# A three-stage kernel whose first feed-forward trades 16 plain chunk products for sets of seven half-size products

## Chip, cores and metric

The kernel runs on one core of one Trainium2 chip. The metric is the device time of one execution in microseconds (us); lower is better.

## What is computed

```
attn = causal attention of q, k, v (4 x 8 heads, 576 tokens, head size 64) with a
       per-position bias min(0, cum[j] - cum[i]), cum the running sum of max(s, 0)
x = attn as 2304 tokens x 512
h = x @ w_in                          # 512 x 2048
x = (h * cos(h)) @ w_out              # 2048 x 512        first feed-forward
xn = x / rms(x) * rms_g
g = xn @ w_gate; v = xn @ w_val       # 512 x 1536 each   second feed-forward
out = (silu(g) * v) @ w_out2          # 1536 x 512
```

Weights of the feed-forwards arrive as 64-bit numbers; the kernel makes 32-bit ones of them (`value`). A feed-forward operand is held as two parts, a rounded one and the rest (`split`: a copy and a subtraction), and each product is three matmuls: high by high, high by low, low by high.

## The kernel before

**Stages.** Attention runs over 16 pairs of heads. The first feed-forward follows, then the second one's gate and value products, then its output product. `T_FF1`, `T_FF2` and `T_OUT` are the times at which the planner sets them.

**Order.** Every instruction is a `plan.op` with an engine (or a choice of two), a cost and a due time. `Plan.order` walks through them once on the host and writes one fixed order for each engine; on the chip each engine follows its own list and waits on semaphores. All DMAs are issued from SyncE (SP). A buffer is reused in the order in which the code asks for it, so the order of uses of a PSUM bank is fixed too.

**First feed-forward.** Tokens go in blocks of 512 (the last of 256). For each block and each of 16 chunks of 128 hidden columns, a tick: `gemm1` (12 matmuls, L737) writes one bank; ScalarE and VectorE make h * cos(h) of it (`Identity` L855, a subtraction L350, `Sin` L857, a multiplication, then a split); `gemm2` (12 matmuls, L743) adds to four accumulator banks and is due 1.6 ticks after its `gemm1`. All 16 + 16 weight chunks lie split in SBUF: those of `w_in` are made during attention, those of `w_out` at the stage's start. When a block is done, `rms_norm` and `rms_store` normalise it (squares L799, a ones-matmul L815, some tiny VectorE steps, the scaling L834) and store it to DRAM.

**Second feed-forward.** Gate and value products are made with seven half-size products for eight: weight pairs `p` and `p + 6` and two halves of 384 tokens form a 2 x 2 block product. `pair_weights` makes the combinations of weights during the first feed-forward, splits them, and stores both parts to DRAM; `load_w` brings them back. `load_x2` combines and splits the activations. One set is seven products (`product`, L985: 6 matmuls of 384 columns each) into four banks, two groups of four banks taking turns:

```
mm(b1, "11", "11", True, 0)
...
mm(b2, "S2", "T2", True, 1)
...
mm(b4, "S3", "T3", True, 2)
...
mm(b3, "S1", "T1", True, 3)
...
last_product = mm(b1, "12", "21", False, 4)
mm(b4, "22", "T4", False, 5)
mm(b3, "S4", "22", False, 6)
```

ScalarE copies b1 out, and VectorE adds the partial sums of the other banks in SBUF tiles `t1`, `t2`, `t3`. The product that writes b4 a second time has two products between itself and the first writing, and so has that of b3. There are 36 sets. The output product (L1126) is of the same seven-product form, with 256 columns a matmul.

## Time and profile before

| | |
|---|---|
| median of 3 runs | 980.69 us (979.43 to 982.83) |
| profiled execution, its own time | 982.97 us |
| profiled execution, span of instructions | 981.2 us |
| TensorE busy | 975.1 us, 99% |
| VectorE, ScalarE, GpSimd busy | 75%, 54%, 12% |
| DMA | 197.49 MB, 201 GB/s over the span |

The span runs from the first to the last instruction of the profiled execution; its own time is 1.8 us longer. Durations below come from that one execution. A line number is that of `kernel.py`; a helper such as `two` (L350) or `copy` (L339, L342) has one line for all its uses.

### The profile page before, as it was taken

Reading aid. Unit: us, or ns where it says so; the run is one execution under the profiler, and the core shown is the slowest. Engines: PE = TensorE matmul, PEld = TensorE weight load, DVE = VectorE, ACT = ScalarE, POOL = GpSimd, SP = SyncE. Lnnn points to the kernel's source line nnn. Section 1 sums busy time; section 2 is a strip of 40 time slices with the busy share of each in tenths; the row PEclk is TensorE's granted clock in tenths of the full one; section 3 lists DMA queues with packets and bytes.
Section 4 is the critical chain, followed back from the end, with each engine's and each line's share of the span. In section 5 each row is a group of like instructions: output and inputs, shape, how many; then the busy total and the mean of one; then the engine's idle time right before and its main releaser. Section 6 shows DMA issues by size and latency. Waiting matters only on the chain.

```text
span 981.2 us, 17344 instructions
## 1 busy us (share of the span) xinstructions
PE 975.1 (99%) x5792; PEld 844.9 (86%) x5792; DVE 735.3 (75%) x1641; ACT 534.7 (54%) x1200; POOL 116.3 (12%) x244
## 2 busy tenths in 40 slices
PE   9999999999999999999999999999999999999998
PEld 5666666788888888888888999999999999999998
DVE  4778777888798889868756988766566579987651
ACT  4999999765566575555544662321221225665540
POOL 2445443021101110101100000000000000000000
PEclk9999999999999999999999999999999999999999
DMA  7799997344355556565442444746556378998761
GB/s 237 249 294 307 316 309 227 125 150 130 123 219 216 189 198 236 195 217 209 173 155 87 131 177 138 242 137 210 174 168 220 108 216 270 286 322 244 214 189 44
DMA packets 131834, 197.49 MB, mean 201 GB/s; under 512 B 13104, under 2 KB 93888, under 8 KB 131744
## 3 DMA queue, kind: packets, MB, share of 16 engines
q1 hardware_dynamic: 131744, 196.38, 61.8%
q8 instruction: 45, 0.74, 0.3%
q14 instruction: 45, 0.37, 0.1%
HBM read 129.67 MB, written 66.67 MB: 200 GB/s over the span
## 4 chain that ended last, share of the span: by engine, by line
PE 98%; ACT 1%; DVE 0%; issue 0%; POOL 0%; ACTq 0%; DVEq 0%; POOLq 0%
PE bank L985 27%; PE bank L737 21%; PE bank L743 20%; PE bank L1126 14%; PE bank L638 5%; PE bank L604 4%; PE bank L554 4%; PE bank L578 2%; ACT Pb L339 1%; PE bank L724 0%; PE bank L706 0%; PE bank L519 0%; PE bank L714 0%; PE bank L815 0%; DVE e L561 0%
## 5 line engine op out<-in xcount | busy, mean ns | idle before, releaser
L350 DVE TENSOR_TENSOR wk<-wk,bank 128x384 f32<-128x384 f32 (+2 forms) x237 | 130.8, 558 | 114.0 <-PE bank L985 40.6
L737 PE MATMUL bank<-xa,wi 128*128 128x512 f32 (+1 forms) x960 | 213.5, 374 | 0.0
L743 PE MATMUL bank<-wg,wr 128*128 128x512 f32 (+1 forms) x960 | 210.7, 371 | 0.0
L737 PEld LDWEIGHTS bank<-xa,wi 128*128 128x128 f32 x960 | 167.9, 188 | 35.4 <-issue 0.3
L743 PEld LDWEIGHTS bank<-wg,wr 128*128 128x128 f32 x960 | 167.7, 188 | 33.6
L985 PE MATMUL bank<-wr,wg 128*128 128x384 f32 x504 | 116.4, 338 | 0.0
L985 PE MATMUL bank<-wi,wg 128*128 128x384 f32 x504 | 115.0, 336 | 0.0
L350 DVE TENSOR_TENSOR wg<-wk,wg 128x512 fp32r<-128x512 f32 (+1 forms) x137 | 82.6, 624 | 13.0 <-ACT wg L339 10.7
L439 POOL TENSOR_SCALAR wk<-wk 128x512 f32<-128x512 f32 x68 | 53.4, 787 | 327.1 <-ACT wk L436 312.4
L855 ACT ACTIVATE wk<-bank,quarter 128x512 int32<-128x512 f32 x72 | 49.3, 685 | 78.5 <-PE bank L737 68.2
L339 ACT ACTIVATE wg<-wk 128x512 fp32r<-128x512 f32 (+1 forms) x123 | 68.0, 571 | 43.2 <-DVE wk L350 30.5
L985 PEld LDWEIGHTS bank<-wr,wg 128*128 128x128 f32 x504 | 91.3, 188 | 0.0
L985 PEld LDWEIGHTS bank<-wi,wg 128*128 128x128 f32 x504 | 89.5, 188 | 0.4
L1126 PE MATMUL bank<-wi,wr 128*128 128x256 f32 x585 | 73.6, 281 | 0.0
L561 DVE CUSTOM_DVE_ANT_0 e<-bank,ce 128x512 f32<-128x512 f32 (+2 forms) x96 | 49.7, 553 | 30.0 <-PE bank L554 18.8
L589 ACT ACTIVATE e<-e,mn 128x512 f32<-128x512 f32 (+3 forms) x128 | 70.4, 558 | 2.7 <-DVE mn L561 2.7
L339 ACT ACTIVATE wk<-bank 128x384 f32<-128x384 f32 (+2 forms) x48 | 23.0, 509 | 89.3 <-PE bank L985 51.1
L1126 PEld LDWEIGHTS bank<-wi,wr 128*128 128x128 f32 x585 | 71.2, 188 | 0.0
L350 DVE TENSOR_TENSOR wk<-wk 128x256 f32<-128x256 f32 (+2 forms) x143 | 66.7, 498 | 3.5 <-ACT wk L799 3.1
L857 ACT ACTIVATE wk<-wk,half_pi 128x512 f32<-128x512 f32 x72 | 51.9, 723 | 30.9 <-DVE wk L350 30.7
L339 ACT ACTIVATE wr<-wr 128x384 fp32r<-128x384 f32 x108 | 54.3, 522 | 23.4 <-DMA wr<-g 11.0
L350 DVE TENSOR_TENSOR wk<-bank,wk 128x512 f32<-128x512 f32 (+1 forms) x82 | 55.1, 673 | 13.1 <-ACT wk L857 12.9
(123 smaller groups left out, 1440.1 us busy)
## 6 DMA issues: line engine op xcount, KB each, us to landing
wk<-in_w_out_dram SPq DMA_DIRECT2D x28, 512.0 KB, 5.0
wr<-g_S SPq DMA_DIRECT2D x54, 192.0 KB, 3.1
qk<-in_qk_dram SPq DMA_DIRECT2D x16, 608.0 KB, 4.6
w_g<-wg SPq DMA_DIRECT2D x18, 512.0 KB, 3.4
w_v<-wg SPq DMA_DIRECT2D x18, 512.0 KB, 5.2
wr<-g SPq DMA_DIRECT2D x48, 192.0 KB, 4.1
g_S<-wk SPq DMA_DIRECT2D x45, 192.0 KB, 2.4
wk<-in_w_in_dram SPq DMA_DIRECT2D x16, 512.0 KB, 5.9
```

The source lines that it names most:

```text
L339: alts.append(("ACT", (act_p if psum else act_s)(n), lambda: act.activation(o(), i(), AF.Copy, scale=scale)))
L350: return plan.op(on("DVE", dve1(n), lambda: dve.tensor_tensor(out=o(), in0=a(), in1=b(), op=op)), r, w, **kw)
L439: plan.op(on("POOL", 660, lambda: pool.tensor_scalar(out=top().bitcast(F32), in0=top().bitcast(F32), scalar1=0.0, scalar2=1.0, op0=ALU.mul ...
L561: plan.op(on("DVE", dve1(w) + 17, lambda t=t, o=o, w=w, i=i, e=e: dve.tensor_tensor_reduce(out=Es[e]()[:, o:o + w], in0=Sp[e]()[:, o:o + w ...
L589: plan.op(on("ACT", act_s(w) + 187, lambda E=E, o=o, w=w, i=i, c=c: act.activation(E()[:, o:o + w], E()[:, o:o + w], AF.Exp, scale=-1.0, b ...
L638: pe.matmul(X()[64 * e:64 * e + 64, lo:hi], vr()[:kk, e, c, :], p[e], start=(c == 0), stop=(c == jobs[-1][0]))
L737: pe.matmul(h, w[:, a, 128 * k:128 * k + 128], x[k // 2][:, k % 2, c, :blk], start=(n == 0), stop=(n == 11))
L743: pe.matmul(acc[t], w[:, c, 128 * t:128 * t + 128], g[a], start=(first and (a, c) == (0, 0) and t % per == 0), stop=(last and (a, c) == (1 ...
L855: plan.op(on("ACT", act_p(512) + 93, lambda u=u, h=h: act.activation(u().bitcast(I32), h(), AF.Identity, bias=quarter)), [h], [u])
L857: plan.op(on("ACT", 628, lambda u=u: act.activation(u(), u(), AF.Sin, scale=-TWO_PI, bias=half_pi)), [], [u], table="sin", prio=O_SIN)
L985: pe.matmul(bank_()[:, :HALF2], G[i]()[:, u, o + 128 * k:o + 128 * k + 128], xs[k]()[:, c, :], start=(first and n == 0), stop=(n == 5), sk ...
L1126: pe.matmul(bk_()[:, col:col + 256], gs[p // 3]()[:, u, 128 * (p % 3):128 * (p % 3) + 128], w3[p][i]()[:, c, o:o + 256], start=(n == 0), s ...
```

## The change

The first layer of the first feed-forward now takes the seven-product form: chunk pairs `p` and `p + 8` and tokens in 3 blocks of two halves of 384 make 24 sets, in an order that takes the first three pairs through all blocks first. The result, h * cos(h), goes to DRAM unsplit (`g1_d`). The second layer then runs as a stage of its own, plain, in 6 units of 384 tokens: per unit 16 steps of 12 matmuls into four banks, each step's operand loaded from `g1_d` and split just before.

A new `winograd` function, used by both feed-forwards, sums partial products in PSUM: ScalarE copies a bank into another bank (`move`) or VectorE adds into one, and the next product accumulates on top. The SBUF tiles for the partial sums go. Cosine, silu and the gate multiplication run on two neighbouring banks with one instruction of 768 elements.

`w_in` pairs 0 to 2 are combined and split during attention (`pair_in`); pairs 3 to 7 are combined, stored unsplit (`pair_store`) and loaded and split later (`pair_load`). `w_out` is converted and stored during the first layer and split in the second layer's first unit. The weights of the second feed-forward are no longer made during the first one and kept in DRAM: each pair is converted, combined and split when its set comes near (`ff2_weights`), and the output weights between sets (`pair_out`). `load_x` makes the activation combinations, from the attention's result for the first feed-forward and from the normalised one for the second. `rms` follows each unit of the second layer and reads three of its banks until its last step. Planner constants and buffer places change along with it.

```
-    def gemm1(h, w, x, blk):
-        n = 0
-        for k in range(4):
-            for a, c in ((0, 0), (0, 1), (1, 0)):
-                pe.matmul(h, w[:, a, 128 * k:128 * k + 128], x[k // 2][:, k % 2, c, :blk], start=(n == 0), stop=(n == 11))
-                n += 1
-
-    def gemm2(acc, g, w, first, last, per):
-        for a, c in ((0, 0), (0, 1), (1, 0)):
-            for t in range(4):
-                pe.matmul(acc[t], w[:, c, 128 * t:128 * t + 128], g[a], start=(first and (a, c) == (0, 0) and t % per == 0),
-                          stop=(last and (a, c) == (1, 0)), skip_group_check=True)
-
...
-            h, u, g = h_bank(j), u_r.new(), g_r.new()
-            for i, f in enumerate(fs):
-                plan.now = tick_at(k)
-                ticks[k] = plan.op(on("PE", 1450 if n0 == 256 else 2815, lambda i=i, w=w1[f], h=h, x=xs[j], n0=n0: gemm1(
...
-            plan.now = tick_at(k) - LEAD_E
-            plan.op(on("ACT", act_p(512) + 93, lambda u=u, h=h: act.activation(u().bitcast(I32), h(), AF.Identity, bias=quarter)), [h], [u])
-            two(u, lambda u=u: u().bitcast(I32), h, 512, [h], [u], psum=True)
-            plan.op(on("ACT", 628, lambda u=u: act.activation(u(), u(), AF.Sin, scale=-TWO_PI, bias=half_pi)), [], [u], table="sin", prio=O_SIN)
-            two(u, h, u, 512, [h], [u], op=ALU.mult, psum=True)
-            copy(lambda g=g: g()[:, 0, :], u, 512, [u], [(g, 0)])
-            two(lambda g=g: g()[:, 1, :], u, lambda g=g: g()[:, 0, :].bitcast(F32), 512, [u, (g, 0)], [(g, 1)])
...
+    def pair_in(d, p, w, pairs, slot, late=True):
+        v1, v2, a22, s, S = pair_sums(w, p, pairs, late)
+        G = slot_of(d, p, slot)
         split(halves_of(G[0], 0, 512), v1, 512, [v1], [G[0]])
+        split(halves_of(G[2], 0, 512), lambda: s()[:, 1:3, :].rearrange("p a b -> p (a b)"), 512, [(s, 1), (s, 2)], [G[2]])
...
+    def pair_store(w, p, pairs, to, late=True):
+        v1, v2, a22, s, S = pair_sums(w, p, pairs, late)
+        load(lambda: to()[:, 0:512], v1, 1 << 18, [v1], [(to, 0)])
+        load(lambda: to()[:, 512:768], a22, 1 << 17, [v2], [(to, 1)])
...
-    def load_w(n):
-        p, d = n // 2, "gv"[n % 2]
-        G = W[d, p] = [w_at[n % 3][i][0].buf(w_at[n % 3][i][1], (2, 512 if i < 3 else 256), F32R) for i in range(4)]
-        for i in range(4):
-            o = load(lambda i=i: G[i]().bitcast(F32), parts_d[d, p][i], 1 << (19 if i < 3 else 18), [parts_d[d, p][i]], [G[i]])
...
+    def winograd(mm, bs):
+        spare = key = spare_r.new()
+        b1, b2, b4, b3 = bs
+        mm(b1, "11", "11", True, 0)
+        mm(b4, "S1", "T1", True, 1)
+        move(half(b2), half(b1), [b1], [b2])
+        move(spare, half(b4), [b4], [key])
+        mm(b2, "S2", "T2", False, 2)
+        mm(b1, "12", "21", False, 3)
+        move(half(b3), half(b2), [b2], [b3])
+        two(half(b2), half(b2), spare, HALF2, [key], [b2], op=ALU.add, psum=True)
+        mm(b3, "S3", "T3", False, 4)
+        last = mm(b2, "S4", "22", False, 5)
+        two(half(b4), half(b3), spare, HALF2, [key, b3], [b4], op=ALU.add, psum=True)
+        mm(b3, "22", "T4", False, 6)
+        return last
+
+    def both(b):
+        return lambda: psum_t[:, b.slot:b.slot + 2, :HALF2]
+
+    def move(o, i, r, w):
+        plan.op(on("ACT", act_p(HALF2), lambda: act.copy(o(), i())), r, w)
+
+    for p in range(3):
+        plan.now = W1_FROM + W1_EACH * p
+        pair_in("i", p, w_in, PAIRS1, p, late=False)
+    w1_d = [dbuf(f"w1_{p}", [128, 1792]) for p in range(3, PAIRS1)]
+    for p in range(3, PAIRS1):
+        plan.now = W1_FROM + W1_EACH * p
...
+    for i in (1, 2, 5, 6):
+        plan.now = T_FF1 - 4000.0
+        bk = bank.new(i)
...
+    def first_set(n, p, b):
+        at = T_FF1 + n * P_SET
+        b1, b2, b3, b4 = (bank.new(i) for i in SETS[n % 2])
+        us = entry((n + 4) % 5)
+        mm = lambda bk, a, x, first, off: (setattr(plan, "now", at + off), product(bk, "i", p, a, b, x, first), setattr(plan, "now", at - LEAD_C))[1]
...
+        def wave(i, x, y):
...
+            dst, src, m, w = (lambda: us()[:, i:i + 2, :]), both(x), 2 * HALF2, [(us, i), (us, i + 1)]
+            plan.op(on("ACT", act_p(m) + 93, lambda: act.activation(dst().bitcast(I32), src(), AF.Identity, bias=quarter)), [x, y], w)
+            two(dst, lambda: dst().bitcast(I32), src, m, [x, y], w, psum=True)
+            plan.op(on("ACT", act_s(m) + 108, lambda: act.activation(dst(), dst(), AF.Sin, scale=-TWO_PI, bias=half_pi)), [], w, table="sin", prio=O_SIN)
+            two(dst, src, dst, m, [x, y], w, op=ALU.mult, psum=True)
+
+        def keep(i, f):
+            load(lambda: g1_d()[:, f, 2 * b * HALF2:2 * (b + 1) * HALF2], lambda: us()[:, i:i + 2, :].rearrange("x a b -> x (a b)"), 1024 * HALF2,
+                 [(us, i), (us, i + 1)], [(g1_d, (f, 2 * b)), (g1_d, (f, 2 * b + 1))], run=3072)
+
...
+        wave(0, b1, b2)
+        wave(2, b3, b4)
+        keep(0, p)
...
+        keep(2, p + PAIRS1)
...
+    for n, (p, b) in enumerate(first_sets):
...
+    def rms(u, bs):
+        st, s, g = st_r.new(), sq_r.new(), hl_r.new()
+        ys = [y_r.new() for _ in range(4)]
+        for k in range(4):
+            q = s if k == 0 else q_r.new()
+            plan.op(on("ACT", act_p(HALF2), lambda k=k, q=q: act.activation(q(), half(bs[k])(), AF.Square)), [bs[k]], [q])
+            if k:
+                two(s, s, q, HALF2, [q], [s], op=ALU.add)
...
+        cut = lambda a: (lambda: g()[:, a, :])
...
+        for k in range(4):
+            v = ys[k]
+            plan.op(on("DVE", dve1(HALF2) + 61, lambda v=v, k=k: dve.scalar_tensor_tensor(
+                out=v(), in0=half(bs[k])() if k else v(), scalar=gcol()[:, k:k + 1], in1=s(), op0=ALU.mult, op1=ALU.mult)), [s, gcol] + [bs[k]] * (k > 0), [v])
...
+    for u in range(2 * NB2):
+        T_U = T_MID + u * EACH
+        bs = [bank.new(i) for i in SETS[u % 2]]
+        for m, f in enumerate(ORDER):
+            w = w2[m]
+            if u == 0:
+                plan.now = T_U + 2108.0 * m - LEAD_O
+                load(lambda w=w: w()[:, 1, :].bitcast(F32), o1_d[f], 1 << 18, [o1_d[f]], [w], run=2048)
+                split(lambda w=w: (w()[:, 0, :], w()[:, 1, :]), lambda w=w: w()[:, 1, :].bitcast(F32), DM, [], [w])
...
+            g = gm[0 if u < 3 else 1 if u < 5 else 2].new()
+            load(lambda g=g: g()[:, 1, :].bitcast(F32), lambda f=f, u=u: g1_d()[:, f, u * HALF2:(u + 1) * HALF2], 512 * HALF2, [(g1_d, (f, u))], [g], run=4 * HALF2)
+            split(lambda g=g: (g()[:, 0, :], g()[:, 1, :]), lambda g=g: g()[:, 1, :].bitcast(F32), HALF2, [], [g])
+
+            def go(g=g, w=w, to=bs, first=(m == 0), last=(m == F1 - 1)):
+                for k in range(4):
+                    for a, c in ((0, 0), (0, 1), (1, 0)):
+                        pe.matmul(to[k]()[:, :HALF2], w()[:, c, 128 * k:128 * k + 128], g()[:, a, :],
+                                  start=(first and a == 0 and c == 0), stop=(last and a == 1), skip_group_check=True)
+
...
+        if u == 2:
+            plan.now = T_U
+            pair_in("g", 0, w_gate, PAIRS2, 2)
+        plan.now = T_U + EACH - LEAD_R
+        rms(u, bs)
...
+    def x_second(b, tmp):
+        plan.now = T_FF2 + (XB0, XB1, XB2)[b]
+        load_x(b, xn_d, lambda k, lo: [(k, lo // HALF2)], tmp, XG2)
+
...
+    def ff2_weights(n):
+        pair_in("gv"[n % 2], n // 2, (w_gate, w_val)[n % 2], PAIRS2, (2, 1, 0)[n % 3])
...
-                two(t2, t1, half(b2), HALF2, [t1, b2], [t2], op=ALU.add, psum=True)
-                mm(b4, "S3", "T3", True, 2)
-                plan.now = at - 3000.0
...
+                mm = lambda bk, a, x, first, off: (setattr(plan, "now", at + off), product(bk, d, p, a, b, x, first), setattr(plan, "now", at - 3000.0))[1]
+                e4 = next_e()
+                last_product = winograd(mm, (b1, b2, b3, b4))
+                    sil = e4
+                    for i, x, y in ((0, b1, b2), (2, b3, b4)):
+                        plan.op(on("ACT", act_p(2 * HALF2), lambda i=i, src=both(x), sil=sil: act.activation(sil()[:, i:i + 2, :], src(), AF.Silu)), [x, y], [(sil, i), (sil, i + 1)], table="silu")
+                    for i, x, y in ((0, b1, b2), (2, b3, b4)):
+                        to = lambda i=i, sil=sil: sil()[:, i:i + 2, :]
+                        two(to, both(x), to, 2 * HALF2, [x, y], [(sil, i), (sil, i + 1)], op=ALU.mult, psum=True)
...
+                        plan.now = T_FF2 + (n + 5 * (m - 2 * p - 3)) * P_SET - LEAD_W
+                        ff2_weights(m)
```

## Rows read from the trace of the kernel before

**Rows 1.** The page: TensorE's busy time, and the chain that ended last by line.
```profile
PE 975.1 (99%) x5792; PEld 844.9 (86%) x5792; DVE 735.3 (75%) x1641; ACT 534.7 (54%) x1200; POOL 116.3 (12%) x244
...
PE bank L985 27%; PE bank L737 21%; PE bank L743 20%; PE bank L1126 14%; PE bank L638 5%; PE bank L604 4%; PE bank L554 4%; PE bank L578 2%; ACT Pb L339 1%; PE bank L724 0%; PE bank L706 0%; PE bank L519 0%; PE bank L714 0%; PE bank L815 0%; DVE e L561 0%
```

**Rows 2.** Busy time by stage (columns in the first line; counts in brackets).
```profile
core 0: us, PE busy (x) PEld busy (x) DVE busy (x) ACT busy (x) POOL busy (x), PEclk, DMA share, GB/s
25.00:162.00 137.00, 136.17 (x1037) 89.28 (x1038) 105.60 (x372) 135.98 (x445) 64.06 (x157) 1.00 0.95 296
162.00:178.70 16.70, 16.57 (x120) 12.34 (x114) 13.28 (x35) 16.35 (x43) 3.21 (x6) 1.00 0.45 125
178.70:578.50 399.80, 399.80 (x1906) 331.93 (x1906) 329.74 (x617) 232.95 (x396) 42.66 (x52) 1.00 0.50 173
360.00:400.00 40.00, 40.00 (x174) 32.33 (x173) 38.09 (x81) 24.81 (x45) 5.76 (x6) 1.00 0.60 218
584.00:843.60 259.60, 259.60 (x1485) 258.67 (x1484) 185.76 (x378) 70.79 (x151) 0.00 (x0) 1.00 0.62 192
```

**Rows 3.** The chain in order of time: start, us, what.
```profile
166.22 2.80 PE bank L737 x12
...
170.75 3.00 PE bank L737 x12
...
223.66 2.81 PE bank L737 x12
226.47 2.77 PE bank L743 x12
...
584.05 259.57 PE bank L985 x1482
```

**Rows 4.** Groups by shape, 200 to 570 us: count, busy us, mean ns, idle before.
```profile
L350 DVE TENSOR_TENSOR wk<-bank,wk 128x512 f32<-128x512 f32 x65 | 44.7, 689 | 10.8 <-ACT wk L857 10.5
...
L442 DVE SCALAR_TENSOR_TENSOR wk<-wk 128x512 int32<-128x512 int32 x48 | 36.5, 760 | 0.4
L440 DVE SCALAR_TENSOR_TENSOR wk<-wk 128x512 int32<-128x512 int32 x48 | 33.8, 704 | 6.6 <-POOL wk L439 6.6
...
L857 ACT ACTIVATE wk<-wk,half_pi 128x512 f32<-128x512 f32 x65 | 46.8, 723 | 26.2 <-DVE wk L350 26.1
```

**Rows 5.** VectorE in order of time: start, us; equal neighbours are merged (x5).
```profile
307.03 1.09 DVE L350 TENSOR_TENSOR wk<-wk 128x256 f32<-128x256 f32 x3
...
308.37 0.68 DVE L350 TENSOR_TENSOR wk<-wk,bank 128x512 f32<-128x512 int32 x1
308.97 0.42 DVE L350 TENSOR_TENSOR wk<-wk 128x256 f32<-128x256 f32 x1
...
598.26 0.55 DVE L350 TENSOR_TENSOR wk<-wk 128x384 f32<-128x384 f32 x1
...
599.19 2.43 DVE L350 TENSOR_TENSOR t<-t 128x384 f32<-128x384 f32 x5
```

**Rows 6.** All engines in order of time, two hand-overs from TensorE to a reader.
```profile
703.79 0.69 PE L985 MATMUL bank<-wi,x 128*128 128x384 f32 x3
703.99 1.14 DVE L350 TENSOR_TENSOR wk<-wk,bank 128x384 f32<-128x384 f32 x2 [1.83 <-PE bank L985]
...
704.84 0.68 PE L985 MATMUL bank<-wi,x 128*128 128x384 f32 x3
705.04 0.49 ACT L339 ACTIVATE t<-bank 128x384 f32<-128x384 f32 x1
```

**Rows 7.** VectorE in order of time, the last block's normalisation.
```profile
584.11 0.45 DVE L818 STREAM_TRANSPOSE wk<-bank 128x256 f32<-128x256 f32 x1
...
588.34 1.67 DVE L834 SCALAR_TENSOR_TENSOR wk<-wk,gcol 128x256 f32<-128x256 f32 x4
```

**Rows 8.** DMA issues by size, us from issue to landing.
```profile
xn_d<-wk SPq DMA_DIRECT2D x16, 256.0 KB, 3.4
wk<-xn_d SPq DMA_DIRECT2D x12, 192.0 KB, 3.8
```

More of the change, by code (lines that the diff above doesn't have):

```diff
@@ L311, in ring @@
         r = Ring(plan, make, n)
-        if where in ("main", "x1", "att"):
+        if where in ("main", "att", "early"):
             for i in range(n):
@@ L900, in pair_weights, with pair_sums @@
-        G = [ws_r.new() for _ in range(4)]
+        return s, [lambda i=i: s()[:, i, :] for i in range(4)]
+    def pair_sums(w, p, pairs, late):
+        v1, v2 = value(w[p], late), value(w[p + pairs], late)
+        s, S = sums()
+        a11, a12, a21, a22 = quarters(v1, v2)
         two(S[1], a21, a22, 256, [v2], [(s, 1)], op=ALU.add)
@@ new lines, in x_first, with next_e @@
+    def x_first(b, tmp):
+        plan.now = (XA0, XA1, XA2)[b]
+        load_x(b, x_d, x_keys, tmp, (XG0, XG0, XG1)[b])
+    x_first(0, (0, 1))
+    x_first(1, (2, 3))
+    g1_d = dbuf("g1_d", [128, F1, NT])
+    turn_e = [0]
+    def next_e():
+        turn_e[0] += 1
+        return entry(turn_e[0] - 1)
+    x_first(2, ())
+    for f in range(F1):
+        plan.now = W2_FROM + W2_EACH * f / 2
+        v = value(w_out[f])
+        load(o1_d[f], v, 1 << 18, [v], [o1_d[f]], run=2048)
+    for i in (1, 2, 5, 6):
+        plan.now = T_FF1 - 4000.0
+        bk = bank.new(i)
+        plan.op(on("PE", 176, lambda bk=bk: pe.matmul(bk()[:, :HALF2], one_r, X[0, "11", 0]()[:, 0, :], start=True, stop=True)), [X[0, "11", 0]], [bk])
@@ L1015, in attention_moe_moe @@
                 at = T_FF2 + n * P_SET
-                if b == NB2 - 1 and 2 * p + (d == "v") + 3 < 2 * PAIRS2:
-                    pass
-                b1, b2, b3, b4 = (bank.new(i) for i in sets[n % 2])
+                b1, b2, b3, b4 = (bank.new(i) for i in SETS[n % 2])
                 n += 1
-                mm = lambda bk, a, x, first, off: (setattr(plan, "now", at + off), product(bk, d, p, a, b, x, first))[1]
-                half = lambda bk: (lambda bk=bk: bk()[:, :HALF2])
-                mm(b1, "11", "11", True, 0)
@@ L1104, in attention_moe_moe @@
             if m == 0:
-                staged[unit] = [bank.new(i) for i in sets[unit % 2]], oo_r.new(), oo_r.new()
+                staged[unit] = [bank.new(i) for i in SETS[unit % 2]], oo_r.new(), oo_r.new()
             banks, o1, o2 = staged[unit]
```

452 lines of the change are left out of this document (176 added, 276 removed).

## The prediction

> **What bounds the kernel now.** I read the page first: TensorE is busy 99% of the span, and the chain that ended last runs through it for 98% [rows 1]. A pipelined matmul makes that share look good, so next come the stages [rows 2] and the chain in order of time [rows 3]. In the first feed-forward TensorE works for all of 399.8 us: a tick of `gemm1` and `gemm2` takes 2.81 + 2.77 us, end to end. In the second one 1482 matmuls of 384 columns take 259.57 us, 0.17515 us each, with no gap. Both stages therefore cost their matmuls, and what removes matmuls there removes time as long as TensorE doesn't begin to wait. Attention is another matter: TensorE 136.2, ScalarE 136.0 of 137 us, DMA 0.95 [rows 2]. There three resources are full together. The granted clock is 1.00, the 2.4 GHz level, in every stretch [rows 2].
>
> **Matmuls removed and added.** Before: 72 ticks (4.5 blocks by 16 chunks) by 5.58 = 401.8 us. After: first layer 24 sets by 42 matmuls = 1008, by 0.17515 = 176.6 us; second layer 6 units by 16 by 12 = 1152, 201.8 us; four matmuls that prepare banks, 0.7 us. Sum 379.1, a saving of 22.7 us. The normalisation keeps its ones-matmuls in kind and in columns (12 of 384 for 8 of 512 and 2 of 256). The profiled execution took 982.97 us; the median, 980.69, is 2.3 lower, and I subtract from the median: 980.7 - 22.7 = 958.0 with no new wait. What waits come is the rest of the question.
>
> **Hand-overs inside a set.** Before, a bank that is written twice has two products between, 2.10 us (6 matmuls are 1.05). Now S2 needs ScalarE's move of the first product, with only S1 between; S3 needs the move of b2, with only 12 between; the last product needs VectorE's sum in b3 and b4, with only S4 between. A reader starts 0.20 us after TensorE goes on to the next product (703.79 to 703.99, 704.84 to 705.04), and ScalarE needs 0.49 for 384 elements out of PSUM [rows 6], VectorE 0.55 [rows 5]. Of 1.05 us that leaves 0.36, 0.36 and 0.30. The fourth, VectorE's b2 + spare after the move, has 2.10 - 0.69 - 0.55 = 0.86. If the engine asked is in the middle of something, TensorE waits, unless its order holds the next set's first two products there (they need a free bank alone), 2.10 us of cover. Bounds: nothing, as in the 259.57 us without a gap [rows 3]; or at each of the three a whole 768-wide operation just begun. From 0.69 at 512 and 0.55 at 384 (0.135 us for 128 more) such an operation is an estimated 0.96 us on VectorE, and `Sin`, 0.72 at 512, about as much [rows 4, 5]: (0.60 + 0.60 + 0.66) by 24 sets = 45 us. In the stage of now VectorE is busy 38.1 of 40 us at its densest while TensorE waits for nothing [rows 2]; the cover should work, so I stay near the lower end: 0.08 a set, 2.0 us. In the second feed-forward the longest operations are as wide but fewer; 0.
>
> **VectorE in the first layer.** Per set two sums of 384 and four operations of 768. By durations (0.55, 0.96): 4.95 us, 24 sets 119. The two later blocks' activations, 44 operations of 384: 24. `w_out`'s 16 conversions by 0.704 + 0.760 [rows 4]: 23. Two late `w_in` pairs (four conversions, eight sums of 0.42): 9. Five loaded pairs' splits (two of 512, three of 256, each): 13. Together 188 of 176.6 us: more than there is. But [rows 5] show that an operation starts before the last has ended: five of 384 last 2.43 us, so (2.43 - 0.55) / 4 = 0.47 apart; 512 wide are 308.97 - 308.37 = 0.60 apart, 256 wide (1.09 - 0.42) / 2 = 0.33, and 768 wide by the same slope 0.87. By spacing: 4.41 by 24 = 106, and 20, 20, 8 and 11: 165, 93%. I take the spacing, at no cost; the excess by durations, 188 - 177 = 11 us, is the other bound. The Trainium skill (Perfetto Trace Analysis, Identifying the Most-Contended Engine) calls occupancy a fair measure of the Vector engine; by that alone the 188 us would decide. The same page (Optimizing Scalar/DVE Operations) says that the write-acknowledge half of an operation overlaps with the next, and the spacing agrees: 0.47 against 0.55.
>
> **Attention.** Its work changes in kind. Gone: the splits of ten of 16 `w_in` chunks, and two blocks' activations. Added: combinations, five pairs' stores, the first blocks' combined activations. Only three pairs and one block are needed when the products start; the rest has 20 us (second block) to 66 us (pair 3, after nine sets) more. VectorE's part before the end, now: 16 conversions 23, 16 splits 11, four operations of 1024 some 5 = 39 us. Then, in step with the need: six pairs' 12 conversions 18, 24 sums 10, three pairs' splits 8, one block's 22 operations 12 = 48 us. Its 9 us more go into 137 - 105.6 = 31 idle ones [rows 2]: 0. If all of it falls inside: +4.6 MB stored, +3.1 MB activations, -3.1 MB not loaded = 4.6 MB at 296 GB/s, 15.6 us. In the last pair `gemm1` fills TensorE now, 5.8 us between 166 and 179 [rows 3], asking nothing of other engines. Then only one set can (the last pair holds four banks), and beyond its first 2.1 us it needs ScalarE, busy 16.35 of 16.7 [rows 2]. Between 0 and 5.8 - 2.1 = 3.7 us; I take 1.0.
>
> **From the second layer to the second feed-forward.** The last unit's `rms` holds banks 4 to 7 until its last scaling; the second set wants them. Now the last product ends at 578.55 (the stage's end in [rows 2]) and the scaling at 588.34 + 1.67 = 590.0 [rows 7]: 11.5 us. The transposing read, after which bank 4 is free, ends at 6.0. TensorE has the first set, 7.36, and one product, 1.05; then S1 waits. Between 0 (products of the third set put there) and 11.5 - 7.4 = 4.1; I take 2.0. The block normalised last is wanted by the fifth set, 29.4 us after: 11.5 + 3.4 (store) + 3.8 (load) [rows 8], about 10 us of combining: 0, with some 2 us if VectorE is late.
>
> **What lies beside.** Second layer: per step (2.10 us) one split on VectorE (0.47) and ScalarE (0.5) and 197 KB, 94 GB/s. Second feed-forward: VectorE by spacing 98 us for sets, some 60 for ten pairs of weights, 23 for the output's and 13 for their splits, 10 for activations = 204 of 265, against 185.8 of 259.6 now [rows 2]; GpSimd's conversion steps fall into a stage where it had nothing to do; DMA +7 MB on 0.62 [rows 2]. On SP's queue the loads of raw weights stand where those of prepared ones stood, with the same stores behind them. All this: 0. Had VectorE not these 61 us free, the sets would pay for the 83 us of weights, less the 53 that go with the partial sums (18 operations of 0.47 a pair of sets before, 5.5 us after, 18 pairs): 30 us.
>
> Sum: 958.0 + 2.0 + 1.0 + 2.0 = **963 us**, own range 957 to 968.
>
> **Rivals.**
> 1. VectorE becomes the bound of the first layer: the 11 us by durations come on top, with the two transitions 958 + 11 + 3 = 972 us. For it: 93% leaves little room, and its order is fixed. Against it: 38.1 of 40 us without a wait now.
> 2. Attention grows. 958 + 15.6 + 4 = 977.6 us, all but no change. For it: ScalarE and DMA are full there. Against it: the due dates allow most of it later.
> 3. Slower: the hand-overs aren't covered. A set's banks come free only 0.2 + 0.9 + 3 by 0.96 = 4.0 us after it (read, `Identity`, subtraction, `Sin`, multiplication), so the next set's early products may not be there to stand in; at the worst 958 + 45 = 1003 us. It decides from 22.7 / 24 = 0.95 us a set, half of its worst. For it: three margins of 0.3 us where there were 1.3. Against it: TensorE can run the other set meanwhile for half of the time.
>
> That the matmuls don't go cannot be: their counts are in the code.
>
> **Numbers.** Forecast 0.70; rivals 0.13, 0.08, 0.09. Changes within 0.3% (2.9 us) can't be told from none here. Faster (below 977.7): 0.70, 0.12 of the first, 0.04 of the second = 0.86. Same: 0.01, 0.03 and 0.01 = 0.05. Slower: 0.01 of the second and 0.08 of the third = 0.09. Range 955 (no wait at all, and the 0.3%) to 976: 0.67 of the forecast, 0.10 of the first rival, 0.03 of the second = 0.80.
>
> **What would show it.** Right: 1008 first-layer matmuls in about 178 us and 1152 in about 202, TensorE's idle time in the first feed-forward below 5 us, attention's period unchanged, a gap of some 2 us after the second layer. Wrong: TensorE idle before products that wait for ScalarE's moves or VectorE's sums, in every set (third rival); VectorE without a pause and TensorE waiting for its 768-wide operations to free banks (first); the first set later than 175 us (second). A granted clock under 1.00 anywhere would say that waits are long.

## The result, and the profile after

The changed kernel takes 970.99 us (969.39 to 971.54), beside it the kernel before 981.76; the ratio is 0.9889, 95% interval 0.9864 to 0.9915. That is 10.8 us faster, where 17.7 were forecast. The 22.7 us of matmuls are gone; new waits give back some 12 us instead of 5.

First the page of the changed kernel: busy times, and the chain that ended last by engine and by line.

```profile
PE 956.8 (99%) x6038; PEld 887.0 (92%) x6038; DVE 756.4 (78%) x1674; ACT 582.3 (60%) x1283; POOL 130.5 (13%) x267
...
PE 78%; DVE 9%; DMA 5%; issue 3%; ACT 2%; SPq 1%; POOL 0%; DVEq 0%; POOLq 0%; ACTq 0%
PE banks L837 36%; PE banks L998 21%; PE banks L1123 12%; DVE wk L347 3%; PE banks L536 3%; PE banks L620 2%; PE banks L586 2%; DVE e L543 1%; PE banks L560 1%; DVE wk L428 1%; SPq L351 1%; DVE banks L347 1%; DMA rb<-rn_d 1%; DMA wk<-in_w_in_dram 1%; DVE wk L430 1%
```

L837 is a set's product, L998 the second layer, L1123 the output, L620 and L586 are attention's P-V and transposes, L869 the moves, L347 every sum, difference and product of two operands on VectorE, L428 and L430 the conversions' two steps. TensorE's busy share is still 99%, but the chain, which ran through TensorE for nearly all of the span [rows 1], now leaves it for 22%. The busy times by stage (columns in the first line) say where:

```profile
core 0: us, PE busy (x) PEld busy (x) DVE busy (x) ACT busy (x) POOL busy (x), PEclk, DMA share, GB/s
25.00:162.00 137.00, 132.94 (x1003) 86.61 (x999) 125.51 (x433) 127.47 (x408) 61.09 (x152) 1.00 0.94 299
207.00:359.40 152.40, 151.64 (x848) 147.51 (x848) 146.61 (x219) 119.57 (x195) 24.81 (x34) 1.00 0.77 272
359.40:577.00 217.60, 217.60 (x1243) 217.09 (x1241) 137.53 (x312) 92.13 (x188) 5.30 (x8) 1.00 0.46 140
577.00:846.00 269.00, 267.70 (x1559) 265.22 (x1558) 216.98 (x412) 137.05 (x260) 20.60 (x27) 1.00 0.67 204
```

Attention (first row, the stretch of the first of [rows 2]): ScalarE fell from 136.0 to 127.5 us, VectorE rose from 105.6 to 125.5, and no engine is full any more: TensorE has 132.9 instead of 136.2; the transfers' share is 0.94 for 0.95. The first layer alone (second row): 848 matmuls by the 0.17515 us of [rows 3] are 148.5 us in 152.4, so 3.9 us are lost, though TensorE counts as busy for 151.6: the modelled end of a matmul covers a short wait. The Trainium skill (Perfetto Trace Analysis, Identifying the Most-Contended Engine) says not to judge by the matmuls' occupancy but by MFU, the share of the peak arithmetic, and by the weight loads' busy share. This trace agrees for matmuls of one width: PEld is 96.8% here against 99.6% in the gapless stage of 384 columns in [rows 2]; in the gapless stage of mostly 512 columns there it is 83%. The second layer (third row) loses nothing: 1243 by 0.17515 are 217.7 us.

How attention's period is read: the first P-V matmul of the first pair and of the fifteenth, in TensorE's order of time (start, us), of the kernel before

```profile
25.49 0.76 PE L638 MATMUL bank<-Pb,vr 128*64 128x320 f32 x4
...
160.72 0.76 PE L638 MATMUL bank<-Pb,vr 128*64 128x320 f32 x4
```

and of the changed kernel, with attention's last P-V, the second layer's first matmul and the place where it runs into the second feed-forward (the products from 563.83 on are already that one's):

```profile
23.16 1.03 PE L620 MATMUL banks<-Pb,vr 128*64 128x320 f32 x6
...
165.78 0.76 PE L620 MATMUL banks<-Pb,vr 128*64 128x320 f32 x4
...
183.84 0.87 PE L620 MATMUL banks<-Pa,vr 128*64 128x256 f32 x8
...
359.25 2.07 PE L998 MATMUL banks<-wz,we 128*128 128x384 f32 x11
...
563.83 6.49 PE L837 MATMUL banks<-wi,wz 128*128 128x384 f32 x36
...
577.60 4.62 PE L837 MATMUL banks<-wi,wg 128*128 128x384 f32 x25 [0.44 <-DVE wk L977]
```

Fourteen periods took 135.23 us (9.66 each) and take 142.62 (10.19). With these rows the two profiled executions (982.97 and 971.15 us) are compared by stage. A stage's own matmuls are counted with it, also where they lie inside a neighbour's time: 5.8 us of `gemm1` and one set of 7.36 us lie inside attention's end, and 13 products of the second feed-forward, 78 matmuls or 13.7 us, before 577.60. So the first feed-forward before is 578.4 - 178.3 + 5.8, and after 577.6 - 184.5 + 7.4 - 13.7.

| stage | before, us | after, us | difference |
|---|---|---|---|
| to the first pair's P-V | 25.5 | 23.2 | -2.3 |
| 14 periods of attention | 135.2 | 142.6 | +7.4 |
| attention's end, without the first feed-forward's matmuls in it | 11.8 | 11.4 | -0.4 |
| first feed-forward | 405.9 | 386.8 | -19.1 |
| second feed-forward and output | 399.4 | 402.1 | +2.7 |

The sum is -11.7, the difference of the last matmul's end (977.8 and 966.1). The first row can't be put down to the change: among the runs below, those that have the changed kernel's instructions in the same order up to there lie between 19.9 and 27.1 us. So attention's body gave back the most. In the first layer, from 184.5 (end of the last P-V) to 359.25 there are 174.74 us for 966 matmuls, 169.2: 5.5 lost. These two, the period and the first layer's loss, are what the experiments are read by: both are differences inside one trace, and neither knows when the kernel began. The loss takes in a wait at attention's end, 0.7 us at 185.54 in this trace.

Two views show the waits behind them. ScalarE's exponentials and copies of `Pb` in 40 to 160 us (by line; busy, mean ns, idle before), of the kernel before

```profile
L589 ACT ACTIVATE e<-e,mn 128x128 f32<-128x128 f32 (+3 forms) x97 | 53.2, 555 | 0.0
L339 ACT ACTIVATE Pb<-bank 128x512 f32<-128x512 f32 (+3 forms) x104 | 36.0, 409 | 0.3 <-PE bank L604 0.3
```

and of the changed kernel, with VectorE's copies of `Pb`:

```profile
L571 ACT ACTIVATE e<-e,mn 128x128 f32<-128x128 f32 (+3 forms) x92 | 51.5, 565 | 5.2 <-DVE mn L543 5.0
L336 ACT ACTIVATE Pb<-banks 128x256 f32<-128x256 f32 (+3 forms) x72 | 29.3, 448 | 2.2 <-PE banks L586 1.6 <-DVE Pb L339 0.6
L339 DVE COPY Pb<-banks 128x64 f32<-128x64 f32 (+1 forms) x20 | 6.2, 345 | 1.1 <-PE banks L586 0.6 <-ACT Pb L336 0.4
```

ScalarE, which hardly ever stood still (119.5 us busy of 120), now waits for VectorE's score passes (L543). It makes 72 copies of `Pb` for 104; 20 are VectorE's now, which had none, and the other 12 fall outside the window. And the first layer's chain in order of time (start, us, what), a stretch in which TensorE isn't the one that is waited for:

```profile
283.83 1.95 PE banks L837 x11
285.82 0.04 issue
285.86 0.48 ACT wk L869
286.34 0.85 ACT wk L911
...
287.21 0.96 DVE wk L347
288.17 0.47 DVE banks L347
...
289.41 0.56 DVE banks L347
289.97 0.89 DVE wk L428
...
304.04 2.03 PE banks L837 x10
```

A move (L869) is followed by `Sin` (L911), that by VectorE's 768-wide operation, the sums into banks and a conversion step: for 18 us VectorE's queue leads, and TensorE follows; the wait that ends with 304.04 is itself only 0.3 us.

### The profile page after: what moved, and what is told of

Read it like the earlier page. It is cut to its first block, busy times and chain, and to the rows that moved or that the text cites. A ratio compares the mean times of both kernels' runs of the same rounds, so it can differ in the third digit from the quotient of the medians.

```text
span 969.4 us, 18247 instructions
## 1 busy us (share of the span) xinstructions
PE 956.8 (99%) x6038; PEld 887.0 (92%) x6038; DVE 756.4 (78%) x1674; ACT 582.3 (60%) x1283; POOL 130.5 (13%) x267
## 4 chain that ended last, share of the span: by engine, by line
PE 78%; DVE 9%; DMA 5%; issue 3%; ACT 2%; SPq 1%; POOL 0%; DVEq 0%; POOLq 0%; ACTq 0%
PE banks L837 36%; PE banks L998 21%; PE banks L1123 12%; DVE wk L347 3%; PE banks L536 3%; PE banks L620 2%; PE banks L586 2%; DVE e L543 1%; PE banks L560 1%; DVE wk L428 1%; SPq L351 1%; DVE banks L347 1%; DMA rb<-rn_d 1%; DMA wk<-in_w_in_dram 1%; DVE wk L430 1%
## 5 line engine op out<-in xcount | busy, mean ns | idle before, releaser
L837 PE MATMUL banks<-wi,wg 128*128 128x384 f32 x882 | 174.5, 337 | 1.7 <-ACT banks L869 1.1
L837 PEld LDWEIGHTS banks<-wi,wg 128*128 128x128 f32 x882 | 154.1, 188 | 6.1 <-ACT banks L869 3.4
L347 DVE TENSOR_TENSOR wg<-wg 128x384 fp32r<-128x384 f32 (+2 forms) x123 | 68.1, 565 | 61.4 <-ACT wg L336 61.2
L837 PE MATMUL banks<-wr,wg 128*128 128x384 f32 x588 | 107.5, 339 | 0.1
L998 PE MATMUL banks<-wg,wr 128*128 128x384 f32 x600 | 106.9, 338 | 0.0
L998 PEld LDWEIGHTS banks<-wg,wr 128*128 128x128 f32 x600 | 105.7, 188 | 0.0
L837 PEld LDWEIGHTS banks<-wr,wg 128*128 128x128 f32 x588 | 103.2, 188 | 1.3 <-ACT banks L869 0.4
L869 ACT COPY banks<-banks 128x384 f32<-128x384 f32 x120 | 56.3, 469 | 78.5 <-PE banks L837 75.0
L347 DVE TENSOR_TENSOR wk<-wk,banks 128x256 f32<-128x256 f32 (+1 forms) x111 | 70.6, 647 | 32.3 <-PE banks L1123 29.1
L347 DVE TENSOR_TENSOR banks<-banks,wk 128x384 f32<-128x384 f32 x120 | 67.0, 559 | 33.7 <-ACT banks L869 22.6
L347 DVE TENSOR_TENSOR wk<-wk 128x256 f32<-128x256 f32 (+1 forms) x194 | 89.3, 490 | 2.7 <-ACT wk L947 0.6
L347 DVE TENSOR_TENSOR wk<-banks,wk 128x768 f32<-128x768 f32 x84 | 79.7, 951 | 5.9 <-PE banks L837 4.2
L837 PE MATMUL banks<-wi,wz 128*128 128x384 f32 x378 | 75.5, 337 | 0.6 <-DVE wk L347 0.5
L837 PEld LDWEIGHTS banks<-wi,wz 128*128 128x128 f32 x378 | 66.2, 188 | 2.3 <-ACT banks L869 1.0
L837 PE MATMUL banks<-we,wg 128*128 128x384 f32 x294 | 67.7, 339 | 0.0
L1123 PE MATMUL banks<-wi,wr 128*128 128x256 f32 x501 | 62.0, 282 | 0.6 <-DVE wi L347 0.6
L1123 PEld LDWEIGHTS banks<-wi,wr 128*128 128x128 f32 x501 | 60.4, 188 | 1.2 <-DVE wi L347 1.0
L543 DVE CUSTOM_DVE_ANT_0 e<-banks,ce 128x512 f32<-128x512 f32 (+2 forms) x96 | 49.8, 544 | 13.0 <-PE banks L536 9.2
L428 DVE SCALAR_TENSOR_TENSOR wk<-wk 128x512 int32<-128x512 int32 x68 | 51.2, 753 | 7.7 <-POOL wk L427 6.6
```

What stands on the lines that cost most here:

```text
L347: return plan.op(on("DVE", dve1(n), lambda: dve.tensor_tensor(out=o(), in0=a(), in1=b(), op=op)), r, w, **kw)
L428: plan.op(on("DVE", 640, lambda: dve.scalar_tensor_tensor(out=top(), in0=low(), scalar=29, in1=top(), op0=ALU.logical_shift_right, op1=ALU ...
L543: plan.op(on("DVE", dve1(w) + 17, lambda t=t, o=o, w=w, i=i, e=e: dve.tensor_tensor_reduce(out=Es[e]()[:, o:o + w], in0=Sp[e]()[:, o:o + w ...
L837: pe.matmul(bank_()[:, :HALF2], G[i]()[:, u, o + 128 * k:o + 128 * k + 128], xs[k]()[:, c, :], start=(first and n == 0), stop=(n == 5), sk ...
L869: plan.op(on("ACT", act_p(HALF2), lambda: act.copy(o(), i())), r, w)
L998: pe.matmul(to[k]()[:, :HALF2], w()[:, c, 128 * k:128 * k + 128], g()[:, a, :], start=(first and a == 0 and c == 0), stop=(last and a == 1 ...
```

## The experiments

Each run is given by its ratio to the kernel before, beside it on the same chip (0.9889 for the changed kernel), with the attention period and the first layer's loss out of its trace, worked out as above. Two ratios with intervals of 0.003 on either side differ for sure only from about 0.004, 4 us. How far a period can be trusted is seen from five traces in which all engines have the same instructions in the same order until the fifteenth P-V is past: the changed kernel, the eighth product, `w_out` light, the sums at the end and the short moves. They show 10.08 to 10.20, 10.15 in the mean.

| run | us | ratio, 95% interval | period, us | first layer's loss, us |
|---|---|---|---|---|
| changed kernel | 970.99 | 0.9889 (0.9864 to 0.9915) | 10.19 | 5.5 |
| eighth product | 997.07 | 1.0143 (1.0105 to 1.0180) | 10.08 | 6.7 |
| `w_out` light | 966.99 | 0.9843 (0.9813 to 0.9873) | 10.17 | 1.9 |
| sums at the end | 964.58 | 0.9825 (0.9791 to 0.9860) | 10.14 | 2.7 |
| late pairs light | 975.77 | 0.9932 (0.9904 to 0.9959) | 10.31 | 8.1 |
| old attention constants | 969.27 | 0.9894 (0.9865 to 0.9924) | 10.58 | 4.2 |
| no late pairs | 974.78 | 0.9943 (0.9922 to 0.9963) | 10.33 | 6.5 |
| before, new order | 988.06 | 1.0081 (1.0059 to 1.0103) | 9.98 | |
| same order, light VectorE | 966.26 | 0.9872 (0.9842 to 0.9902) | 10.04 | 5.0 |
| same order, light transfers | 968.54 | 0.9887 (0.9859 to 0.9914) | 10.12 | 4.7 |
| short moves | 967.80 | 0.9867 (0.9841 to 0.9894) | 10.20 | 4.0 |
| before, new shares | 983.47 | 1.0030 (1.0012 to 1.0048) | 10.26 | |
| sums on GpSimd | 967.54 | 0.9867 (0.9844 to 0.9891) | 10.46 | 2.4 |

### What limits the first layer

**An eighth product.** Product 11 is done twice in each of the 24 first-layer sets.

```diff
...
-        mm(b1, "11", "11", True, 0)
+        for _ in range(1 + twice):
+            mm(b1, "11", "11", True, 0)
...
```

> The changed kernel (970.99 us) with product 11 of each of the 24 first-layer sets done twice, so that its second run overwrites the first: 144 matmuls more, 24 x 1.05 = 25.2 us of TensorE, nothing more for other engines. If the first layer is bound by TensorE with waits of its own beside it (hand-over theory: the waits are inside the sets, and the extra product stands ahead of all of them), the time rises by 23 to 25 us, to some 995. If VectorE sets the pace there (VectorE theory), the 25 us give it room and the waits of some 5 us go: a rise of 19 to 21 us, to some 991. A rise below 10 us would say that the eighth product was never what the time hung on.

The ratio rose by 0.0254, 24.9 us; 24 by 6 matmuls by 0.17515 are 25.2. The added work costs itself, so TensorE sets the first layer's pace, and VectorE has nothing like the 11 us of excess in which such work would hide. The added time is free time for VectorE, yet the loss doesn't go. Busy times in 210 to 387 us, nearly all of this kernel's first layer:

```profile
210.00:387.00 177.00, 175.69 (x988) 171.97 (x987) 147.64 (x217) 121.41 (x196) 26.56 (x34) 1.00 0.68 234
```

By the gapless 0.17515 us, 988 matmuls are 173.0 us of 177, so 4.0 are lost with VectorE busy for 83% of the time; the changed kernel loses 3.9 of 152.4 us with VectorE at 96%. How full VectorE is can't be the whole reason.

**`w_out` light.** VectorE's two conversion steps of `w_out`'s 16 chunks, all in the first layer, are left out.

```diff
-        v = value(w_out[f])
+        v = value(w_out[f], short=True)   # returns before the two steps
```

> The changed kernel with VectorE's two steps of each of the 16 conversions of w_out left out (the weights of the second layer are then wrong); loads, stores, the ScalarE and GpSimd steps stay. VectorE has 16 x 1.46 = 23 us less in and around the first layer. VectorE theory: the waits of the first layer (5.4 us beyond its matmuls) go to 1 or 2, the time falls by 3 to 5 us. Hand-over theory: VectorE is asked too late in the set whatever else it does, the time falls by less than 1.5 us.

The loss fell from 5.5 to 1.9 us. VectorE's busy time in 207 to 350 us, of the changed kernel

```profile
207.00:350.00 143.00, 142.38 (x799) 138.89 (x798) 137.23 (x205) 110.22 (x179) 24.81 (x34) 1.00 0.76 265
```

and of this one:

```profile
207.00:350.00 143.00, 142.90 (x812) 141.28 (x811) 119.69 (x176) 112.38 (x183) 24.40 (x34) 1.00 0.80 281
```

In the changed kernel 799 matmuls are 139.9 us of 143, so 3.1 are lost there. 17.5 us less of VectorE (third busy time) give 13 matmuls more, 2.3 us, most of it. VectorE is at 84% now, but it was at 83% with the eighth product: what counts is that these steps no longer stand ahead of results that TensorE wants. That they did is argued, not shown, as leaving out instructions changes the planned order too, from 230 us on. Late pairs light, the old attention constants and no late pairs, whose first layers were planned anew with VectorE at 135 to 136 of the 143 us, lost 4.2 to 8.1 us, so a new order alone isn't seen to bring 1.9.

**Sums at the end.** The three moves and two sums of each set follow its last product, in both feed-forwards. They then copy banks that further products have gone into, so the sums aren't the reference's; count, kind and size of the instructions stay.

```diff
...
         mm(b3, "22", "T4", False, 6)
+        move(half(b2), half(b1), [b1], [b2])
+        move(spare, half(b4), [b4], [key])
+        move(half(b3), half(b2), [b2], [b3])
+        two(half(b2), half(b2), spare, ...)
+        two(half(b4), half(b3), spare, ...)
```

> The changed kernel with the same three moves and two sums of each set, in both feed-forwards, but behind the set's last product, so that no product waits for one of them (the sums are then wrong). The work of ScalarE and VectorE is the same. Hand-over theory: the waits inside the sets go, 4 to 7 us less, some 965. VectorE theory: no change or some us more, since the banks come free later: 969 to 976.

The loss fell to 2.7 us with VectorE as full as ever:

```profile
207.00:350.00 143.00, 142.87 (x815) 142.33 (x814) 138.50 (x208) 113.06 (x183) 25.80 (x34) 1.00 0.79 277
```

In this stretch 815 matmuls, 142.7 us, leave 0.3 lost, for 3.1 in the changed kernel. What is left of the 2.7 lies ahead of it, most of it one wait of the first set for a copy of attention's:

```profile
183.40 6.51 PE L837 MATMUL banks<-wi,wg 128*128 128x384 f32 x36 [1.06 <-ACT xu L336]
```

So inside the stage nearly all of the loss is paid where products wait inside a set: a full VectorE costs next to nothing there when no product waits for it. Whether for the moves or for the sums, the next run tells.

**Short moves.** Each instruction keeps its place on every engine; the moves of the first layer copy 32 columns for 384, so the sums lack the other columns.

```diff
...
-        winograd(mm, (b1, b2, b4, b3))
+        winograd(mm, (b1, b2, b4, b3), HALF2 if n < 2 else 32)   # columns of the moves
```

> The changed kernel with every instruction in its place on every engine; only the three moves of each first-layer set (from the third set on) copy 32 columns instead of 384, 0.47 us each in the changed kernel (the output is not the reference's). VectorE's work is the same. The first layer loses 5.5 us beyond its 966 matmuls of 0.17515 us in the changed kernel. Hand-over theory (TensorE waits for moves and sums between the products): a move is over some 0.2 to 0.25 us sooner, the loss falls to 2 to 3.5 us and the time by 2 to 4 us to 967 to 969. VectorE theory (its queue of 96 per cent busy delays the sums and the waves): the loss stays at 4.5 to 6 us and the time within 1.5 us of 971.

The moves by line (durations min/median/max in ns) went from the 469 ns of the changed kernel to 170:

```profile
L870 ACT COPY banks<-banks x40: 170/170/196, 207.0 to 351.4; 128x32 f32<-128x32 f32 x40
```

The loss is 4.0 us. Three traces in which the first layer's order is untouched show 5.5, 5.0 and 4.7, so 0.3 us sooner in three places of each set is worth some 1 us, less than the 2 to 3.5 of the hand-over theory and more than the VectorE theory allowed. The profile names the moves as TensorE's releaser (1.1 us of L837's idle time); it names what came last, not why the move came late. What remains is the wait for VectorE's sums; that follows from the runs taken together, as no run has the sums alone made short.

### What lengthens attention

**Late pairs light.** For weight pairs 3 to 7, VectorE's conversion steps and sums are left out; the transfers stay.

> The changed kernel with VectorE's steps left out for the five w_in pairs that are stored and come back later: ten conversions and 20 sums, some 23 us of VectorE, most of it during attention; the stores keep their bytes (the weights of these pairs are then wrong). If attention lost its 4 us to the VectorE work that was added (VectorE theory), its last matmul comes 3 to 4 us earlier than 184.7 and the time falls by 3 to 5 us. If attention lost them to DMA (as many bytes here) or to the planner's other constants, the end of attention moves by less than 1 us.

It went the other way: slower, if barely beyond the intervals, period 10.31. VectorE is busy for 111.8 us in 25 to 162 us instead of 125.5. With instructions gone the planner wrote another order, from 76 us on, and here the order counts for more than the 13.7 us taken away. The next two have a new order as well.

**Old attention constants.** The planner's constants for attention (priorities, period, weights of the engines) are those of the kernel before.

```diff
-    WEIGH = {"PE": 1.0, "ACT": 1.0, "DVE": 2.31, "POOL": 0.67, "SP": 1.0}
+    WEIGH = {"PE": 1.0, "ACT": 1.0, "DVE": 2.02, "POOL": 1.00, "SP": 1.0}
-KEEP_MODE = 1671.0
+KEEP_MODE = 1000.0
-P_ATT, ... = 10949.0, ...
+P_ATT, ... = 10726.0, ...
...
```

> The changed kernel with the planner constants of attention set back to those of the kernel before (order of its steps, their period, the weights by which copies are given to VectorE and ScalarE). Attention's mean period over its pairs is 9.66 us before and 10.19 us in the changed kernel, some 7 us in all. Theory A (the new order and the new shares of the engines make the longer period): the period comes back to 9.7 to 9.8 us with ScalarE near 29.9 of 30 us, and the time falls by 4 to 7 us against the changed kernel, to 964 to 967. Theory B (the added work in attention makes it, above all the DMA traffic of the pair sums and of the first blocks' loads, at a DMA share of 0.94 to 0.96): the period stays at 10.1 to 10.3 us and the time within 2 us of 971.

A miss: period 10.58 with ScalarE at 113.9 of 120 us, and no change in the time. The old constants don't bring the old period back once the new work is in; with the new work the new ones have the shorter period, 10.19.

**No late pairs.** Pairs 4 to 7 are not loaded, converted, summed or stored; their products read pair 3's sums.

> The changed kernel without the loading, conversion, sums and stores of weight pairs 4 to 7 (the products of these pairs read pair 3's sums; the output is not the reference's). It takes about 7.7 MB of transfers and some 16 us of VectorE out of attention. Theory B (DMA): the period falls from 10.19 to 9.7 us or so and the time by 4 to 7 us to 964 to 967. Theory A (order and shares): the period stays at 10.0 to 10.3 us and the time within 2 us of 971.

10.33 and slower, with the DMA share down from 0.94 to 0.87. Neither theory had that; it says only that in a new order less work can cost more.

**Before, new order.** The kernel before with attention's constants of the changed one, no other edit.

> The kernel before with attention's planner constants (order, period, engine weights) of the changed kernel and nothing else. Theory A (order and shares make the longer period): its attention slows by about 0.5 us a pair, the time rises by 4 to 8 us to 986 to 990. Theory B (added DMA work): attention's period stays at 9.7 us and the time within 2 us of 982.

Here the order and the engines' shares are alone, and they cost: the ratio is 1.0081, 7.9 us, and 9.98 for 9.66 makes 4.5 us of it. Attention's end is 2.2 us longer, but it holds a third tick of `gemm1`, 2.8 us, that the first feed-forward no longer has to do, so that is no loss. The last matmuls of the two profiled executions are 4.6 us apart; where the rest of the 7.9 lies isn't shown. Part of it may be the clock: from 11.3 to 18.1 us, in the opening, the granted clock is 0.50 (1.2 GHz), and the mean over the execution is 0.996 to 0.997 in all four runs, for 0.998 to 1.000 in the kernel before. The same wait appears in ScalarE's group, in a kernel whose work is unchanged:

```profile
L589 ACT ACTIVATE e<-e,mn 128x128 f32<-128x128 f32 (+3 forms) x96 | 52.9, 556 | 5.5 <-DVE mn L561 5.4
L339 ACT ACTIVATE Pb<-bank 128x512 f32<-128x512 f32 (+3 forms) x64 | 26.5, 453 | 3.5 <-PE bank L604 3.2
```

**Before, new shares.** Only the weights of the engines and `KEEP_MODE`.

> The kernel before with only the planner's weights of the engines (VectorE 2.31 for 2.02, GpSimd 0.67 for 1.00) and the bound on switching from the changed kernel; the order's priorities and the period stay. With all of attention's constants it was 8.3 us slower than before (attention's period 9.98 instead of 9.66 us, the last pair 2.2 us longer). If the shares (copies moved from ScalarE to VectorE) make the longer period: 984 to 988, period 9.8 to 10.0. If the priorities make it: within 2 us of 981, period 9.7.

The ratio makes 2.9 us of the 7.9. Its mean period of 10.26 holds one first pair of 13.1 us in the profiled execution, in which TensorE, after standing idle for 1.63 us up to 29.11, ran for 3.4 us at a granted clock of 0.50:

```profile
30.90:34.30 3.40, 3.24 (x12) 2.19 (x14) 2.10 (x11) 3.19 (x11) 2.58 (x6) 0.50 1.01 371
```

The other thirteen average 10.04, against 9.63 before and 9.91 with all of the new constants. So the shares lengthen the period by themselves; by the time they are a part, by the period the whole, and what the priorities add stays open.

**Same order, light VectorE.** All instructions of the changed kernel in their places; conversion steps and sums of pairs 1 to 7 work on 32 columns.

```diff
-            out=top(), in0=low(), scalar=29, in1=top(), ...
+            out=top()[:, :c], in0=low()[:, :c], scalar=29, in1=top()[:, :c], ...
-        two(S[1], a21, a22, 256, ...)
+        two(t(S[1]), t(a21), t(a22), 256, ...)    # t: the first c columns
```

> The changed kernel with every instruction in its place on every engine; only VectorE's conversion steps and pair sums of weight pairs 1 to 7 (all within attention) work on 32 columns instead of 512 or 256, which takes some 14 x 2 x 0.7 + 28 x 0.4 = about 30 us of VectorE out of attention (the output is not the reference's). Theory A1 (in VectorE's order these steps stand ahead of score passes that ScalarE waits for): ScalarE's waits for the score pass shrink from 5 us in 40 to 160 us to under 2, attention's period falls from 10.19 to 9.7 to 9.9 us, and the time by 4 to 7 us to 964 to 967. Theory A2 (the order itself, latencies between score pass, exponential and copies, whoever has time): the period stays at 10.0 to 10.2 us, the time within 2 us of 971. Theory B (transfers): the same as A2.

**Same order, light transfers.** The same, with one sixteenth of the bytes in the raw loads of pairs 2 to 7 and the stores of pairs 4 to 7.

> The changed kernel with every instruction in its place on every engine; only the loads of the raw weights of pairs 2 to 7 and the stores of pairs 4 to 7 move one sixteenth of their bytes (some 9 MB fewer in attention; the output is not the reference's). Theory B (a DMA share of 0.94 to 0.96 makes the bias rows, the factor and the blocks' loads late): the period falls from 10.19 to 9.7 to 9.9 us and the time by 4 to 7 us to 964 to 967. Theories A1 and A2: the period stays at 10.0 to 10.2 us, the time within 2 us of 971.

The period is 10.04 with the light VectorE and 10.12 with the light transfers. The second lies among the 10.08 to 10.20 of the five traces with unchanged attention, the first 0.04 below the lowest of them: against their mean it is 1.6 us over 14 pairs, against the lowest 0.5, and attention's end is 0.9 us shorter. With VectorE at 96.5 of 120 us, about what it had before, ScalarE still waits for the score passes:

```profile
L571 ACT ACTIVATE e<-e,mn 128x128 f32<-128x128 f32 (+3 forms) x98 | 54.5, 559 | 4.1 <-DVE mn L543 4.0
```

So the transfers aren't shown to cost anything, and VectorE's added work costs some 0.5 to 1.6 of the 7.4 us; by the ratio neither can be told from nothing. Most of the lengthening stays when the work is made light and its order is kept.

**Sums on GpSimd.** The sums at the end, and attention's pair sums on GpSimd. Its expectation says that it computes the reference; with the sums at the end it can't, for the reason given there.

> The changed kernel with the moves and sums of each set after its last product, as in the kernel with the sums at the end (964.6 us), and the pair sums of the weights in attention on GpSimd (busy 53 of 120 us) instead of VectorE (109 of 120 us). It computes the reference. If VectorE's work stands in attention's way: 961 to 964 us and a period of 10.0 to 10.1 us; if GpSimd's queue delays the masks that the score passes wait for: 966 to 972 and a period of 10.3 us or more.

0.8 us each on GpSimd for 0.45 on VectorE, period 10.46: no gain in attention, while the first layer repeats the small loss (2.4) of the sums at the end.

Of the runs that leave nothing out, none is faster than the changed kernel; the one with the old attention constants can't be told from it.

## Why the prediction was right, and where it was short

**Matmuls removed: right.** The first layer has 1008 and the second 1152, at 0.17515 us where nothing is waited for; the first feed-forward is 19.1 us shorter, against 18.7 forecast (22.7 less 2.0 for the hand-overs and 2.0 for the transition, which lies in the same row). The eighth product shows from the other side that matmuls are the price there. The agreement is partly luck: the hand-overs cost more, and the sum for the kernel before was 1.8 us short. Its 72 ticks took 403.6 us, not 401.8, mostly because a matmul of 256 columns takes more than half of one of 512 (start, us, of the kernel before):

```profile
521.13 2.81 PE bank L737 x12
...
526.71 2.88 PE bank L737 x24
```

**Hand-overs, 2.0 us, and VectorE in the first layer, 0: together 5.5 us measured, and the split was wrong.** The two aren't separate terms. Within 207 to 350 us, 2.8 of 3.1 us go when no product waits for a move or a sum, with VectorE as full as before: TensorE loses where a product waits inside a set for another engine's result. 2.3 go when `w_out`'s steps are taken out of VectorE's queue, some 1 with sooner moves. The queue's fullness as such isn't it, since the eighth product at 83% lost as much as the changed kernel at 96%. By spacing the prediction had VectorE 93% full and let that cost nothing, with the 11 us by durations as the other bound; the truth lies between. Its cover from the kernel before, 38.1 of 40 us without a wait, doesn't carry over: there a product that takes VectorE's results, `gemm2`, is due 1.6 ticks after its `gemm1`, 8.9 us, and here a single product of 1.05 us lies between.

**Attention's body, 0: the step that failed.** It measured 7.4 us. The argument counted VectorE's added work into idle time and bounded the rest by transfers. With the order kept, VectorE's added work is some 0.5 to 1.6 us of it and the transfers nothing that can be told. What it left out is that a planner spreads new work by moving old work: in 25 to 162 us VectorE is busy 19.9 us longer, where 9 were counted, and copies of `Pb` went there from ScalarE. New order and shares alone lengthen attention in the kernel before, by 4.5 us, with the same wait of ScalarE for the score passes. They don't explain the changed kernel by themselves: there the old constants make the period longer still (10.58). Nor is it that VectorE and ScalarE, at 91 and 93% in 40 to 160 us, are nearly full together: with VectorE made light, at 80%, the period is 10.04. How the 7.4 us divide between the added instructions, their order and the shares, and which priorities do it, is open.

**Attention's end, 1.0: it measured -0.4. The transition, 2.0: it measured 0.4** (the row at 577.60): 13 products of the second feed-forward are put before the gap, where the prediction had seven and one, so it comes out near the lower of the two bounds named. **Second feed-forward, 0: +2.7.** Some 0.5 us lie at 758 us behind a late load of `w_val` and 1.3 at 845 behind a late load of the output's weights; the remaining 0.9 is spread thin and wasn't traced.

**The rivals.** The waits of the first layer are the third rival's, in front of products that need a move or a sum, but at 0.2 us a set instead of 0.95, and work of VectorE's that stands ahead of the sums is part of what makes them. The first rival, VectorE as the bound, is refuted by the eighth product. The second came true in its place and by half its price (7.4 of 15.6), though not by its mechanism, the transfers; nor did its sign show, since the first set began at 169.5 us and not after 175. Attention, first layer and second feed-forward cost 13.6 us more than their terms; the shorter transition and end and the 1.8 us above took back 4.8, which is luck.

## What to carry to other kernels

Where the order of work is planned, an edit re-plans its neighbours: price not only the work added to a stage but what the plan moves there, and see in the trace whether the engine that was full without a pause now waits. To find out what a piece of work costs in such a stage, keep each instruction where it is and make it small; leaving it out measures a new order instead. And see first how far executions with the same order differ: here 0.12 us a pair, as much as one of the effects looked for. A queue that is 96% full costs next to nothing as long as nobody waits for a particular entry in it, and one at 83% cost as much here as one at 96% when somebody did.

## What the runs showed of the hardware that was not expected

TensorE's busy time hides short waits: 848 matmuls worth 148.5 us are shown as 151.6 busy, since a matmul's modelled end (0.337 us mean) reaches past the next one's start. Counting matmuls by the gapless 0.17515 us finds the loss, and the weight loads' busy time, 147.5 us, points to it.

The opening up to the first P-V takes 19.9 to 27.1 us in single executions, and 23.2, 20.0 and 27.1 in three kernels whose instructions have the same order up to there (the changed one, the one with light VectorE work and the eighth product). A gain of a few us is therefore read from inside a trace rather than from its end.
